# Quarter-array products with v in an attention and MLP kernel, with new product orders and a last product in three PSUM banks

## The chip, the core and the metric

One NeuronCore of a Trainium2 chip runs the whole program. The metric is the device time of one execution in microseconds (us), the median of several runs. Engines are named as the profile names them: PE (TensorE matmul), PEld (TensorE weight load), DVE (VectorE), ACT (ScalarE), SP (SyncE, which issues all DMAs here).

## The reference

Sigmoid attention over 8 batches and 12 heads of 448 positions and 64 dimensions, then an MLP with a sigmoid-gated activation over the 3584 tokens (768 wide, 2048 hidden):

```python
def _attn_ref(q, k, v):
    S = q.shape[2]                                  # q, k, v: (8, 12, 448, 64)
    scores = 1.0 / np.sqrt(64) * np.matmul(q, k.transpose(0, 1, 3, 2)) - np.log(S)
    attn = 1.0 / (1.0 + np.exp(-scores))
    return np.matmul(attn, v).astype(np.float32)

def _moe_ref(x, w_in, w_out):                       # w_in (768, 2048), w_out (2048, 768), both float64
    h = x @ w_in
    g = h * (1.0 / (1.0 + np.exp(-1.702 * h)))
    return (g @ w_out).astype(np.float32)
```

## The kernel before

The kernel is straight-line code. A planner (`Plan.run`) holds all tasks with their costs and dependencies, takes tasks engine by engine in the order in which they could begin, and so writes an instruction order for PE, ACT, DVE and SP; each engine then works its list in order, waiting on semaphores.

**Attention** comes first. Heads are taken in pairs (64 dimensions each, so two heads fill 128 partitions), and two pairs make a unit; there are 24 units. In a unit (`attention`, from L665) PE does, for each of the two pairs, three chunks of 128 key positions: `scores` (L568, matmuls L578), each chunk into one PSUM tile of two banks, one bank per head. ACT takes the sigmoid of each tile (L564). The last 64 key positions of both pairs share one tile: `scores_left` (L586, L594), on 64x64 quarters of the array. Then come the products with v: `values` (L601, L609) takes all 128 key positions of a chunk in one pass of 128 rows by 64 columns, the two heads side by side in the two column halves, and adds up the three chunks of one pair in one bank of a tile; `values_left` (L615, L622) adds the last 64 positions to it on quarters. One copy of 896 columns (`to_x`, L639, by ACT at L646 or by DVE at L647) takes the tile of two banks out, and SP stores it to DRAM.

PSUM has four tiles of two banks in this stage, q0 to q3, used in turn: a unit takes eight places (`held_ += 8`), seven for scores and one for the products with v, so a score tile waits for the reader of the tile four places earlier.

Beside this DVE and ACT round q and k to a leading and a remaining part (`round_and_rest`, L443 to L449), and decode the 64-bit weights (`decode`, L488 to L507).

**The first block** of 512 tokens (`first_block`) is an ordinary MLP: `up(n)` makes hidden tiles h in q0 (the second in q1), ACT the activation (`graw`, L829), and `down(n)` adds products o_q into q1, q2, q3, in that order of column groups.

**The other six blocks** are done three at a time (`triple`), each with a scheme of 20 products per matrix on sums of inputs (`SEQUENCES` lists the 40 products of a triple, as (matrix, product)). A product is 36 matmuls of 512 columns (L773) into one of two PSUM tiles of four banks, h0 and h1, in turn. DVE and ACT round its input into a pair (`gp`, `xp`, L987 to L999), seed its tile from a sum so far (L1087, L1089), copy it out (L1129) or add it up (L1163). The last product of all is copied to the output one column group at a time (`store`, L1195), from one tile.

Of the kernel before, what the change touches and what calls it, by code (L numbers as in the profile page):

```python
# [19 lines left out]
P = 128  # L20
# [8 lines left out]
    pair=2, wsplit=4, q0=1, q1=1, q2=1, q3=1, h0=1, h1=1,  # L29
# [10 lines left out]

SIGNAL, DRAIN, OVERLAP = 0.05, 0.17, {"ACT": 0.1, "DVE": 0.08}
# [10 lines left out]
SEQUENCES = ([(0, 19), (0, 8), (0, 10), (0, 18), (0, 2), (0, 16), (0, 12), (0, 1), (0, 14), (0, 15), (0, 11), (0, 7), (0, 17), (0, 4), (0, 0), (0, 5), (1, 8), (0, 9), (0, 3), (1, 4), (1, 12), (0, 13), (1, 3), (1, 18), (0, 6), (1, 16), (1, 9), (1, 10), (1, 2), (1, 19), (1, 14), (1, 15), (1, 17), (1, 7), (1, 1), (1, 13), (1, 11), (1, 0), (1, 5), (1, 6)], [(0, 18), (0, 19), (0, 14), (0, 10), (0, 3), (0, 12), (0, 13), (0, 2), (0, 1), (0, 5), (0, 11), (0, 17), (0, 7), (0, 9), (0, 15), (0, 0), (0, 6), (1, 2), (1, 9), (1, 0), (0, 16), (1, 3), (0, 4), (1, 5), (0, 8), (1, 10), (1, 16), (1, 4), (1, 15), (1, 8), (1, 13), (1, 19), (1, 17), (1, 12), (1, 1), (1, 6), (1, 18), (1, 14), (1, 11), (1, 7)])  # L52
# [15 lines left out]
class Task:  # L68
    def __init__(self, emits, costs, deps):
        self.emits, self.costs, self.deps = emits, costs, list(deps)  # L70
        self.ready, self.left, self.then, self.key = 0.0, 0, [], None
        self.begun, self.alone = False, True
        self.holds, self.landing, self.anytime, self.spare = [], LANDING, False, 0


class Buffer:
    def __init__(self):
        self.users, self.tile, self.until, self.slot, self.open, self.kind = [], None, 0.0, None, 0, None


class Plan:
# [3 lines left out]
    def buffer(self, tag):  # L85
        b, ring = Buffer(), self.rings.setdefault(tag, [])
        b.turn = len(ring) % BUFS[tag]
        ring.append(b)
# [11 lines left out]
    def either(self, costs, emits, deps=(), uses=()):  # L100
        t = Task(emits, costs, deps)
        for b in dict.fromkeys(uses):
            b.users.append(t)
        self.tasks.append(t)
        return t

    def run(self, streams):
# [43 lines left out]
        def since(t):  # L151
            when = t.ready
# [21 lines left out]
        def pe():  # L174
            if current:
                return (None if current[0].left else max(free["PE"], current[0].ready)), None
# [6 lines left out]
            for s, unit, due in heads:  # L183
# [4 lines left out]
                for t in first:  # L188
                    when = max(when, t.ready - before)
# [7 lines left out]
        while count < len(self.tasks):  # L197
# [4 lines left out]
            for i, (e, pool) in enumerate(pools.items()):  # L202
                pools[e] = pool = [t for t in pool if not t.begun]
                if pool:
                    options.append((max(free[e], min(since(t) for t in pool)), i + 1, e))
# [8 lines left out]
            else:  # L214
                now = [t for t in pools[e] if since(t) <= when]
# [4 lines left out]
                    if c.key < min(t.key, doing + SOON) and since(c) < when + PATIENCE * t.costs[e]  # L220
                ]
                if soon:
                    t = min(soon, key=lambda t: t.key)
                    when = max(when, since(t))
# [16 lines left out]
            else:  # L241
                free[e] = end - OVERLAP[e]
            for b in t.holds:
# [82 lines left out]
def sigmoid_attention_mlp(ctx: ExitStack, tc: tile.TileContext, qk, v, w, out):  # L326
# [62 lines left out]
    def make(b, tag, shape, dtype, name):  # L389
# [4 lines left out]
        if tag in ("h0", "h1") and tag not in spaces:  # L394
            for t in ("q1", "q0") if tag == "h0" else ("q3", "q2"):
                psum[t].close()
            banks(tag, "left" if tag == "h0" else "right")
        if late:
# [62 lines left out]
    def decode(n):  # L461
# [18 lines left out]
        plan.early.append((load, firsts[min(2 + pair, len(firsts) - 1)]))  # L480
# [87 lines left out]
    def scores(n, c, t_s, s, place):  # L568
# [14 lines left out]
        t = task("PE", (0.7, 0.61, 0.61)[c] if n else 0.9, emit, t_s, [ps, s])  # L583
        return t, sigmoid(f"a{n}_{c}", a, ps, t), a

    def scores_left(n, sources, place):  # L586
# [12 lines left out]
        t = task("PE", 0.8, emit, [t for ts, _ in sources for t in ts], [ps, *(b for _, b in sources)])  # L599
        return t, sigmoid(f"a{n}_{NC}", a, ps, t, "al"), a  # L600

    def values(n, c, t_a, a, t_v, vr, ps):

        def emit():
            if ps.tile is None:
                make(ps, ps.tag, [P, 2, 512], F32, f"av{n}")
            for j, cols in enumerate(halves_of_rows):
                at = ((n % 2 * 2 + j) * NC + c) * D
                nc.tensor.matmul(  # L609
                    ps.tile[cols, n % 2, :S], lhsT=vr.tile[:, at : at + D], rhs=a.tile[:, j],  # L610
                    start=c == 0, stop=False, skip_group_check=True,
                )

        return task("PE", (0.8, 0.75, 0.75)[c], emit, [t_a, t_v], [ps, a, vr])

    def values_left(t_a, a, t_v, vr, ps):
# [659 lines left out]
```

## Time and profile before

| | us |
|---|---|
| median of 3 runs | 1055.24 (1053.51 to 1055.38) |
| span of the profiled execution | 1051.2 |
| PE busy | 1038.1 (99%) |
| DVE busy | 841.9 (80%) |
| ACT busy | 552.7 (53%) |
| DMA, mean over the span | 258 GB/s |

The span is the time from the first to the last instruction of the one execution that was profiled; no device time of that execution is given beside it, so the 4.0 us between the span and the median are taken to lie around the span in every run. Busy shares are means over the span, and a wait by PE is what its busy time leaves out.

### The profile page before, as it was taken

The numbers are of one execution on the slowest core, as the hardware profiler recorded it, in microseconds if no ns is written. First come the engines' busy times: TensorE is split into PE (matmuls) and PEld (weight loads), VectorE is DVE, ScalarE is ACT, GpSimd is POOL, SyncE is SP. The second block draws the span as 40 slices with busy tenths as digits, with TensorE's granted clock in tenths as the row PEclk, the third lists the DMA queues.
The fourth block names the chain that finished last, engine by engine and source line by source line (L and its number), as shares of the span: only waits on it lengthen the run. The fifth ranks groups of instructions, "written<-read, shape, count | busy, mean of one in ns | idle before, by whom it ended". The sixth has DMA issues, their size and how long they took to land.

```text
span 1051.2 us, 13595 instructions
## 1 busy us (share of the span) xinstructions
PE 1038.1 (99%) x5300; PEld 778.9 (74%) x5300; DVE 841.9 (80%) x741; ACT 552.7 (53%) x512; POOL 0.2 (0%) x4
## 2 busy tenths in 40 slices
PE   9999999999999999999999999999999999999997
PEld 5545555555788888888887888888888888788886
DVE  5989789873999766788998989999875596888784
ACT  7888788886564423533554434342443263434342
POOL 0000000000000000000000000000000000000000
PEclk9999999999999999999999999999999999999999
DMA  9999988973999996757556666959766545545765
GB/s 358 388 377 361 342 312 308 344 262 135 336 401 373 372 383 225 256 186 243 193 176 219 233 198 196 295 197 372 274 222 199 184 147 180 153 148 158 234 203 186
DMA packets 114704, 271.44 MB, mean 258 GB/s; under 512 B 10320, under 2 KB 80080, under 8 KB 112592
## 3 DMA queue, kind: packets, MB, share of 16 engines
q1 hardware_dynamic: 114640, 270.57, 73.4%
q8 instruction: 42, 0.69, 0.3%
q14 instruction: 22, 0.18, 0.1%
HBM read 185.60 MB, written 84.93 MB: 257 GB/s over the span
## 4 chain that ended last, share of the span: by engine, by line
PE 91%; DVE 3%; DMA 3%; ACT 2%; issue 1%; SPq 0%; ACTq 0%; DVEq 0%
PE p L773 55%; PE av L609 11%; PE sc L578 9%; PE h L773 6%; PE o_q L773 6%; PE av L622 2%; PE sc L594 2%; DMA c<-wc 1%; ACT gp L987 1%; DVE o L1130 1%; SPq L417 0%; DVE gp L999 0%; DVE gs L716 0%; ACT o L1129 0%; DMA qkraw<-qk 0%
## 5 line engine op out<-in xcount | busy, mean ns | idle before, releaser
L773 PE MATMUL p<-gp,w 128*128 128x512 f32 x1440 | 329.2, 389 | 2.5 <-DVE gp L999 1.1
L773 PE MATMUL p<-xp,w 128*128 128x512 f32 x1440 | 327.8, 389 | 1.0 <-DVE xp L999 1.0
L773 PEld LDWEIGHTS p<-gp,w 128*128 128x128 f32 x1440 | 269.8, 188 | 60.6 <-DVE gp L999 2.0
L773 PEld LDWEIGHTS p<-xp,w 128*128 128x128 f32 x1440 | 270.2, 188 | 57.5 <-DVE xp L999 1.4
L564 ACT ACTIVATE a<-sc,bias 128x896 f32<-128x896 f32 x168 | 153.6, 1025 | 17.9 <-PE sc L578 17.9
L609 PE MATMUL av<-a,vraw 128*64 128x448 f32 x576 | 113.5, 543 | 0.0
L578 PEld LDWEIGHTS sc<-qk 64*128 64x128 f32 x846 | 77.7, 184 | 23.3 <-issue 16.2
L609 PEld LDWEIGHTS av<-a,vraw 128*64 128x64 f32 x576 | 39.2, 137 | 72.6 <-issue 49.5
L578 PE MATMUL sc<-qk 64*128 64x448 f32 x846 | 92.0, 368 | 0.9 <-DVE qk L449 0.9
L999 DVE TENSOR_TENSOR gp<-h,gp 128x2048 fp32r<-128x2048 f32 x31 | 70.9, 2288 | 9.2 <-ACT gp L987 8.8
L1129 ACT COPY h<-p 128x2048 f32<-128x2048 f32 x18 | 33.7, 1874 | 82.6 <-PE p L773 53.2
L773 PE MATMUL o_q<-g,w 128*128 128x512 f32 x288 | 66.5, 389 | 1.2 <-ACT graw L829 1.2
L773 PE MATMUL h<-x,w 128*128 128x512 f32 x288 | 66.6, 390 | 1.0 <-ACT x L646 1.0
L987 ACT CAST gp<-h 128x2048 fp32r<-128x2048 f32 x23 | 44.0, 1913 | 43.5 <-PE p L773 36.2
L1163 DVE TENSOR_TENSOR h<-h,p 128x2048 f32<-128x2048 f32 x23 | 52.1, 2284 | 17.6 <-PE p L773 10.4
L773 PEld LDWEIGHTS h<-x,w 128*128 128x128 f32 x288 | 54.0, 188 | 13.0 <-ACT x L646 1.8
L773 PEld LDWEIGHTS o_q<-g,w 128*128 128x128 f32 x288 | 54.0, 188 | 12.8 <-ACT graw L829 1.6
L1129 ACT COPY o<-p 128x1536 f32<-128x1536 f32 x18 | 25.9, 1443 | 59.5 <-PE p L773 19.2
L449 DVE TENSOR_TENSOR qk<-qkraw,qk 128x896 fp32r<-128x896 f32 x47 | 50.9, 1089 | 6.7 <-ACT qk L443 5.9
L716 DVE TENSOR_TENSOR h<-h,h 128x2048 f32<-128x2048 f32 x24 | 54.7, 2284 | 0.1
L736 ACT CAST wc<-ws 128x384 fp32r<-128x384 f32 (+1 forms) x57 | 32.1, 579 | 39.5 <-DVE ws L716 25.3
L987 ACT CAST xp<-x 128x1536 fp32r<-128x1536 f32 x19 | 28.1, 1480 | 39.2 <-PE p L773 31.4
(108 smaller groups left out, 969.9 us busy)
## 6 DMA issues: line engine op xcount, KB each, us to landing
w<-c SPq DMA_DIRECT2D x140, 384.0 KB, 4.3
w<-c SPq DMA_DIRECT2D x52, 768.0 KB, 4.7
w<-w SPq DMA_DIRECT2D x16, 1536.0 KB, 9.7
c<-wc SPq DMA_DIRECT2D x56, 384.0 KB, 5.6
qkraw<-qk SPq DMA_DIRECT2D x47, 448.0 KB, 6.4
vraw<-v SPq DMA_DIRECT2D x24, 448.0 KB, 6.5
c<-wc SPq DMA_DIRECT2D x14, 768.0 KB, 7.1
c<-w SPq DMA_DIRECT2D x28, 384.0 KB, 3.9
```

Source lines behind the costliest of these rows:

```text
L449: lambda: nc.vector.tensor_tensor(lo(), src(), hi().bitcast(F32), op=ALU.subtract),
L564: nc.scalar.activation(a.tile, ps.tile[:, :, :S], AF.Sigmoid, bias=bias, scale=scale)
L578: nc.tensor.matmul(ps.tile[:, j, :S], lhsT=src[kk][rows, S + c * P : S + (c + 1) * P], rhs=src[qq][rows, :S], start=i == 0, stop=i == len( ...
L594: nc.tensor.matmul(ps.tile[cols, j, :S], lhsT=src.tile[rows, S + NC * P :], rhs=src.tile[rows, :S], start=True, stop=True, skip_group_chec ...
L609: nc.tensor.matmul(ps.tile[cols, n % 2, :S], lhsT=vr.tile[:, at : at + D], rhs=a.tile[:, j], start=c == 0, stop=False, skip_group_check=True,)
L716: return task("DVE", cost, lambda: nc.vector.tensor_tensor(out(), x(), y(), op=op), deps, uses)
L736: t_hi = on_either((act(n), lambda: nc.scalar.copy(into()[:, 0], node.view())), (cast(n), lambda: nc.vector.tensor_copy(into()[:, 0], node ...
L773: nc.tensor.matmul(ps, lhsT=ws[:, a, c * P : (c + 1) * P], rhs=x[:, d, k], start=start and i == 0 and j == 0, stop=stop and i == len(todo) ...
L987: t_hi = on_either((act(n), lambda: nc.scalar.copy(part(0)(), node.view())), (cast(n), lambda: nc.vector.tensor_copy(part(0)(), node.view())),
L999: nc.vector.tensor_tensor(part(1)(), node.view(), part(0)().bitcast(F32), op=ALU.subtract)
L1129: t = on_either((act(self.n), lambda: nc.scalar.copy(view(), node.view())), (dve(self.n), lambda: nc.vector.tensor_copy(view(), node.view())),
L1163: nc.vector.tensor_tensor(view(), x.view(), y.view(), op=ALU.add if s0 == s else ALU.subtract)
```

## The change

Five things are changed.

1. **Quarters.** `values` now issues four matmuls of 64x64 for a chunk: the two halves of its 128 key positions go through the two row halves of the array, into the two banks of a tile. So each pair of heads has a PSUM tile of its own, with two partial sums. `values_left` moves in before the last two chunks, and adds to one bank of each tile.
2. **Taking out.** `to_x` now does, for each of the two tiles, an ACT copy of one bank (448 columns) and a DVE addition of the other bank to it. A unit takes nine PSUM places in place of eight.
3. **The planner** has new costs for these tasks, lets engines that touch the same PSUM tile take turns (`clear`), and gives the weight loads a later rank.
4. **Orders.** New `SEQUENCES` for the two triples; in the first block the o_q column groups go to q2, q3, q1 in place of q1, q2, q3; in the first unit `scores_left` goes between the scores of the two pairs.
5. **The last product** goes into three PSUM tiles of one bank each (z0, z1, z2), each seeded by an ACT instruction, and each copied out by itself (`end`).

```diff
     def values(n, c, t_a, a, t_v, vr, ps):
-            for j, cols in enumerate(halves_of_rows):
-                at = ((n % 2 * 2 + j) * NC + c) * D
-                nc.tensor.matmul(
-                    ps.tile[cols, n % 2, :S], lhsT=vr.tile[:, at : at + D], rhs=a.tile[:, j],
-                    start=c == 0, stop=False, skip_group_check=True,
-                )
-        return task("PE", (0.8, 0.75, 0.75)[c], emit, [t_a, t_v], [ps, a, vr])
+            for h, rows in enumerate(halves_of_rows):
+                for j, cols in enumerate(halves_of_rows):
+                    at = ((n % 2 * 2 + j) * NC + c) * D
+                    nc.tensor.matmul(
+                        ps.tile[cols, h, :S], lhsT=vr.tile[rows, at : at + D], rhs=a.tile[rows, j],
+                        start=c == 0, stop=c == NC - 1 and (n % 2 == 1 or h == 1), skip_group_check=True,
+                    )
+        return task("PE", 0.76, emit, [t_a, t_v], [ps, a, vr])
...
     def to_x(b, p, ends, pair):
+        for k, (t, ps) in enumerate(zip(ends, pair)):
+            def lower(k=k, ps=ps):
+                rows()
+                nc.scalar.copy(xb.tile[:, k], ps.tile[:, 1, :S])
+            c = task("ACT", act(S), lower, [t], [xb, ps])
+            done.append(task("DVE", dve(S), lambda k=k, ps=ps: nc.vector.tensor_tensor(
+                xb.tile[:, k], ps.tile[:, 0, :S], xb.tile[:, k], op=ALU.add), [c], [xb, ps]))
...
-            held_ += 8
-            ps = two_banks(held_)
+            held_ += 9
+            pair = [two_banks(held_ - 1), two_banks(held_)]
...
-            unit = [*run, left[0], *both]
+            unit = [*run, left[0], *both] if n > 1 else [*run[:NC], left[0], *run[NC:], *both]
...
-                for c, (tag, at) in enumerate((("q1", 0), ("q1", 1), ("q2", 0), ("q2", 1), ("q3", 0), ("q3", 1))):
+                for c, (tag, at) in enumerate((("q2", 0), ("q2", 1), ("q3", 0), ("q3", 1), ("q1", 0), ("q1", 1))):
...
+            def end(self, r, tag):
...
+                for i in range(NJ):
+                    bank = buffer(f"z{i}")
...
+                    t = task("ACT", act(T), seed, [*acc.done, *over], [bank, acc.b])
...
+                done = products(self.m, r, g_sums, G_SUMS[1], GB, NJ, 1, (None, tag, True), [], apart)
```

What PE does from the last scores of the second unit on, before (sc are score tiles, a their sigmoids, av the tile of the products with v, L594 and L622 the quarters for the last 64 positions):

```order
L578 MATMUL sc_2_377<-qk_3_320 128x448 x6
L594 MATMUL sc_3_389<-qkraw_2_232 64x448 x2
L594 MATMUL sc_3_389<-qkraw_3_234 64x448 x2
L609 MATMUL av_397<-a_0_347,vraw_2_244 64x448 x2
L609 MATMUL av_397<-a_1_366,vraw_2_244 64x448 x2
L609 MATMUL av_397<-a_2_375,vraw_2_244 64x448 x2
L609 MATMUL av_397<-a_0_386,vraw_2_244 64x448 x2
L609 MATMUL av_397<-a_1_395,vraw_2_244 64x448 x2
L609 MATMUL av_397<-a_2_405,vraw_2_244 64x448 x2
L622 MATMUL av_397<-a_3_415,vraw_2_244 64x448 x4
```

The products with v were of one form and the quarters of another around them. The same place on PE now:

```order
L593 MATMUL sc_2_390<-qk_3_302 128x448 x6
L609 MATMUL sc_3_400<-qkraw_2_230 64x448 x2
L609 MATMUL sc_3_400<-qkraw_3_232 64x448 x2
L626 MATMUL av_407<-a_0_357,vraw_2_234 64x448 x4
L626 MATMUL av_407<-a_1_369,vraw_2_234 64x448 x4
L626 MATMUL av_407<-a_2_387,vraw_2_234 64x448 x4
L626 MATMUL av_433<-a_0_398,vraw_2_234 64x448 x4
L639 MATMUL av_407<-a_3_422,vraw_2_234 64x448 x2
L639 MATMUL av_433<-a_3_422,vraw_2_234 64x448 x2
L626 MATMUL av_433<-a_1_405,vraw_2_234 64x448 x4
L626 MATMUL av_433<-a_2_431,vraw_2_234 64x448 x4
```

A matmul of this list is two instructions on the chip. Everything from `scores_left` to the end of the unit is now of the 64x64 form, there are two av tiles, and the first is complete two groups before the end.

What DVE now does around the end of a later unit (x_2_0 is the result of a unit, its av tiles the two that PE filled; x_0_768 is input of the first block, read back from DRAM; w and expo belong to the decoding of weights):

```order
L464 TENSOR_TENSOR qk_3_1029<-qkraw_3_905,qk_3_1029 128x896
L517 TENSOR_SCALAR w_13_1059<-w_13_924 128x1536
L499 TENSOR_SCALAR expo_1065<-w_13_924 128x1536
L671 TENSOR_TENSOR x_2_0_1067<-av_1023,x_2_0_1067 128x448
L464 TENSOR_TENSOR x_0_768<-x_0_768 128x1536
L671 TENSOR_TENSOR x_2_0_1067<-av_1049,x_2_0_1067 128x448
L515 TENSOR_TENSOR expo_933<-expo_933,sign_931 128x1536
```

Each unit now has two such additions (L671) on DVE, each behind an ACT copy (L668); the second can stand behind work of another kind.

The end of the program on ACT, before (p_4_7 is the last product's tile, o its output):

```order
L1129 COPY o_4_7972<-p_4_14_7878 128x1536
L1089 ACTIVATE p_4_7_7983<-o_2_7620 128x1536
L1195 ACTIVATE o_2_8035<-p_4_7_7983 128x512 x3
```

Seed, matmuls and copies were of one tile. The same place on ACT now (p_4_14_0 to p_4_14_2 are the three banks):

```order
L762 CAST w_4_14_0_8360<-w_4_14_0_8360 128x768
L1155 ACTIVATE p_4_14_0_8384<-o_4_7816 128x512
L762 CAST w_4_14_1_8362<-w_4_14_1_8362 128x768
L1155 ACTIVATE p_4_14_1_8399<-o_4_7816 128x512
L1155 ACTIVATE p_4_14_2_8402<-o_4_7816 128x512
L1167 ACTIVATE o_4_8433<-p_4_14_0_8384 128x512
L1167 ACTIVATE o_4_8433<-p_4_14_1_8399 128x512
L1167 ACTIVATE o_4_8433<-p_4_14_2_8402 128x512
```

The seed and the copies are of a tile per column group now, where one tile served all three.

## Rows read from the trace of the kernel before

**Rows 1.** Page: the span; busy time of PE, its share and instructions.
```profile
span 1051.2 us, 13595 instructions
PE 1038.1 (99%) x5300; PEld 778.9 (74%) x5300; DVE 841.9 (80%) x741; ACT 552.7 (53%) x512; POOL 0.2 (0%) x4
```

**Rows 2.** Waits of PE over the whole span: us in total, times, longest.
```profile
PE o_q L773 <- ACT graw L829: 1.2, 1, 1.2
PE p L773 <- DVE gp L999: 1.1, 2, 0.9
...
PE h L773 <- ACT x L646: 1.0, 1, 1.0
PE p L773 <- DVE xp L999: 1.0, 1, 1.0
PE sc L578 <- DVE qk L449: 0.9, 1, 0.9
PE p L773 <- ACT o L1195: 0.7, 1, 0.7
PE p L773 <- DMA w<-c: 0.6, 1, 0.6
```

**Rows 3.** A stretch of the attention: us, busy time (instructions) of each engine, clock, DMA share, GB/s.
```profile
26.00:208.00 182.00, 182.00 (x1350) 95.02 (x1350) 159.29 (x168) 154.44 (x159) 0.00 (x0) 1.00 0.93 347
```

**Rows 4.** PE timeline of one attention unit: start, us, instructions.
```profile
61.79 0.98 PE L594 MATMUL sc<-qkraw 64*64 64x448 f32 x8
62.71 4.73 PE L609 MATMUL av<-a,vraw 128*64 128x448 f32 x24
67.37 0.98 PE L622 MATMUL av<-a,vraw 64*64 64x448 f32 x8
68.28 3.91 PE L578 MATMUL sc<-qk 64*128 64x448 f32 x36
72.12 0.98 PE L594 MATMUL sc<-qkraw 64*64 64x448 f32 x8
```

**Rows 5.** Weight loads (PEld) in the same unit.
```profile
63.13 0.14 PEld L609 LDWEIGHTS av<-a,vraw 128*64 128x64 f32 x2 [0.23 <-issue]
...
66.52 0.14 PEld L609 LDWEIGHTS av<-a,vraw 128*64 128x64 f32 x2 [0.23 <-issue]
67.36 0.21 PEld L622 LDWEIGHTS av<-a,vraw 64*64 64x64 f32 x8 [0.70 <-ACT sign L488]
```

**Rows 6.** L622's matmuls in two short stretches of that unit.
```profile
67.35:67.75 0.40, 0.38 (x4) 1.00 1.11 367
67.75:68.25 0.50, 0.50 (x8) 1.00 1.36 338
```

**Rows 7.** PE timeline of the first unit.
```profile
3.94 3.31 PE L578 MATMUL sc<-qkraw 64*128 64x448 f32 x12
8.15 2.09 PE L578 MATMUL sc<-qk 64*128 64x448 f32 x18 [0.90 <-DVE qk L449]
...
16.66 3.90 PE L578 MATMUL sc<-qk 64*128 64x448 f32 x36
```

**Rows 8.** Groups by line and shape: busy us, mean ns; idle before, releasers.
```profile
L1195 ACT ACTIVATE o<-p 128x512 f32<-128x512 f32 x3 | 1.7, 595 | 13.8 <-PE p L773 13.8
L646 ACT COPY x<-av 128x896 f32<-128x896 f32 x12 | 10.9, 908 | 22.1 <-PE av L622 22.1
L647 DVE COPY x<-av 128x896 f32<-128x896 f32 x12 | 13.1, 1089 | 5.5 <-PE av L622 5.5
L739 DVE TENSOR_TENSOR wc<-ws,wc 128x384 fp32r<-128x384 f32 x48 | 25.5, 551 | 0.7 <-ACT wc L736 0.6
L507 DVE SCALAR_TENSOR_TENSOR w<-w,expo 128x1536 f32<-128x1536 f32 x16 | 28.0, 1751 | 0.1
```

**Rows 9.** Timeline of the end, PE and ACT.
```profile
1042.69 3.01 PE L773 MATMUL p<-gp,w 128*128 128x512 f32 x12 [0.75 <-ACT o L1195]
1045.74 1.09 ACT L1195 ACTIVATE o<-p 128x512 f32<-128x512 f32 x2 [3.10 <-PE p L773]
```

More of the change, by code (lines that the diff above doesn't have):

```diff
@@ L87, in buffer @@
         b.turn = len(ring) % BUFS[tag]
+        b.bank = tag in BANKS
         ring.append(b)
@@ L149, in run, with clear, since @@
         at, current, doing = [0, 0], [], 0
-        def since(t):
-            when = t.ready
+        def clear(t, e):
+            return max([end for b in t.banks for by, end in b.busy.items() if by != e], default=0.0)
+        def since(t, e):
+            when = max(t.ready, clear(t, e))
             if "SP" in t.costs and t.key > doing + PRESSING:
@@ L242, in run @@
                 free[e] = end - OVERLAP[e]
+            for b in t.banks:
+                b.busy[e] = max(b.busy.get(e, 0.0), end + SIGNAL)
             for b in t.holds:
@@ L397, in make @@
             banks(tag, "left" if tag == "h0" else "right")
+        if tag[0] == "z" and "z0" not in spaces:
+            psum[last_of[0]].close()
+            banks("z0", "left" if last_of[0] == "h0" else "right")
+            spaces["z1"] = spaces["z2"] = spaces["z0"]
         if late:
@@ L479, in decode @@
         load.landing += 1.5
-        plan.early.append((load, firsts[min(2 + pair, len(firsts) - 1)]))
+        plan.early.append((load, firsts[min(4 + pair, len(firsts) - 1)]))
         def exponent():
@@ L689, in attention @@
             if n % 2:
-                left = scores_left(n, [first, (t_q, qkr)], held_ + 7)
-            chunks = [scores(n, c, [t_s] if n else t_q[: c + 1], s, held_ + 1 + n % 2 * NC + c) for c in range(NC)]
+                left = scores_left(n, [first, (t_q, qkr)], held_ + (7 if n > 1 else NC + 1))
+            at = held_ + 1 + n % 2 * NC + (n == 1)
+            chunks = [scores(n, c, [t_s] if n else t_q[: c + 1], s, at + c) for c in range(NC)]
             if n % 2 == 0:
@@ L859, in first_block @@
             down(n)
-        for k in range(2):
+        for k in (1, 0):
             b = plan.slot()
@@ L1178, in store @@
             k, n = divmod(i, 3)
-            into, bank = out[one + n, k * NJ : (k + 1) * NJ].rearrange("j p t -> p j t"), node
-            parts = [slice(0, NJ)]
+            into = out[one + n, k * NJ : (k + 1) * NJ].rearrange("j p t -> p j t")
+            b, view, done = node.b, node.view, node.done
             if kind == "psum":
-                last = one + 3 == NB and all(left < 0 for left in nets[1].left.values())
-                parts = [slice(j, j + 1) for j in range(NJ)] if last else parts
@@ L1184, in store @@
                 b, view = nets[1].slot(("out", i))
-                node, ends = Node(b, view, []), node.each if last else node.done
+                if sign > 0:
+                    done = [on_either((act(XB), lambda: nc.scalar.copy(view(), node.view())),
+                                      (dve(XB), lambda: nc.vector.tensor_copy(view(), node.view())), done, [b, node.b])]
+                else:
+                    done = [task("ACT", act(XB), lambda: nc.scalar.mul(view(), node.view(), -1.0), done, [b, node.b])]
@@ L1219, in triple @@
             places[i] = onto
-            nets[m].product(r, onto)
+            if one + 3 == NB and i == len(sequence) - 1:
+                plan.rings[onto[1]].pop()
+                nets[m].end(r, onto[1])
+            else:
+                nets[m].product(r, onto)
         return [u for p in sequence for u in units_of[p]]
```

144 lines of the change are left out of this document (80 added, 64 removed).

## The prediction

> **What bounds the kernel now.** I read the page first, then the waits of PE, then timelines of PE at the places that the change touches. The page gives PE 1038.1 of 1051.2 us [rows 1]; what is left is 13.1 us. The waits of PE explain about half of it: eight short ones, among them 1.0 before the first h product, 1.2 before the first o_q product, 0.9 in the first unit and 0.7 in the last product [rows 2]; most of the rest is the end, after PE's last matmul at about 1045.7 (42.69 plus 3.01) [rows 9]. In the attention, from 26 to 208 us, PE is busy for all of 182 us, with the clock at its full 2.4 GHz (granted 1.00) [rows 3]. So nothing that DVE, ACT or DMA do there ends a wait of PE, and a gain must come out of PE's own work, or out of the named waits.
>
> The timeline of one unit shows where PE's work has slack [rows 4]. From one `scores_left` to the next (61.79 to 72.12) a unit takes 10.33 us. Between 61.79 and 68.28, 6.49 us, stand 0.92 for the scores of the last 64 positions, 4.66 for the 24 instructions of `values`, and 0.91 for the eight of `values_left`, each counted from start to start.
>
> **What a change of form costs.** Within `values` the loads of weights step in pairs, ten rows from 63.13 to 66.52, so 3.39 us for nine steps, 0.377 each [rows 5]: two column halves run beside each other for 0.377 us. Twelve such steps are 4.52, and 4.66 is 0.14 more. The quarters of `values_left` are eight instructions in 0.91 us. Four of them run in the first 0.40 us of that group, and all eight are in flight in the next half [rows 6], so four run beside each other; two steps of 0.377 are 0.754, and 0.91 is 0.16 more. I read the 0.14 to 0.16 as the price of changing from one form of matmul to another, and take 0.15.
>
> **The change, part by part.**
>
> *Quarters.* A chunk was four instructions in two steps of two; it becomes eight in two steps of four. That halves nothing: the columns that stream are the same, so a chunk keeps 0.754 us if the steps stay at 0.377. What goes is changes of form. `scores_left`, six chunks and `values_left` are now one run of eight groups of the 64x64 form: 8 x 0.754 + 0.15 = 6.18 us against 6.49, a gain of 0.31 a unit. In 23 units (the first has another order) it is 7.1 us. Bounds of a group in the run: 0.754 from below, since no row shows a faster step, and 0.91 from above, the group that stands alone [rows 4]. I take the lower end: the eight loads of a group start and end within 0.21 us [rows 5], which a step of 0.377 a half can cover. The two ends go into the range and into a rival.
>
> The Trainium skill speaks against more and smaller matmuls: "TensorEngine Tiling (Array Packing)", section Instruction Overhead, gives about 60 cycles of overhead for each. By an estimate from that page, 25 ns at 2.4 GHz for each of the 576 added instructions would be 14.4 us if they were paid one after another, and the sum would come out slower than before. The group that stands alone does not bear this out: its eight instructions take 0.16 us over two steps, and the 24 of the other form take 0.14 over twelve [rows 4].
>
> *First unit.* PE waits 0.90 us there for the first rounded q and k, from about 7.25 to 8.15 [rows 7]. `scores_left` needs only loaded q and k, not rounded ones, and is put into this gap: 0.9 us.
>
> *The first h product* waits 1.0 us for the copy of the last av tile, because both use q0 [rows 2]. With nine places a unit the last two tiles stand in q0 and q1, and the one in q0 is complete two groups, 1.5 us, before the attention ends. ACT needs 0.54 for its copy (595 ns for 512 columns [rows 8], less 64 columns at about 0.83) and DVE 0.62 for its addition (between 551 ns at 384 columns and 1089 at 896 [rows 8]), 1.2 together; q0 is free in time. Gain 1.0 us.
>
> *The first o_q product* waits 1.2 us for `graw` [rows 2], the activation that reads h from q1, where o_q began. It now begins in q2. Gain 1.2 us.
>
> *The last product.* PE stops 0.75 us between its second and third column groups, for ACT's copy out of the same tile, and after PE's last matmul ACT makes two copies in 1.09 us, the first of which could not start before [rows 9]. With a tile per group the stop goes, 0.7, and one copy of 0.60 stays after the end: 0.5 less. The seeds are three ACT instructions of 0.6 [rows 8] and lie beside the product before. Gain 1.2 us, provided that the pair and the weights of the last product, now rounded behind two additions on DVE, are ready.
>
> *Taking out.* A unit gets two copies on ACT (1.08) and two additions on DVE (1.24), and loses one copy, which alternated between ACT at 908 ns and DVE at 1089 [rows 8]: 0.45 and 0.54 on the mean. ACT rises by 0.63 a unit, DVE by 0.70. Before, ACT is busy 154.4 and DVE 159.3 of 182 us [rows 3], 8.76 and 9.03 in a unit of 10.33; now 9.4 and 9.7 in a unit of 10.02. Both still fit, so I cost this at nothing; the cover is 0.6 us of ACT and 0.3 of DVE a unit. If it is gone, PE waits at the fourth score tile of the next unit, which takes the place of the second av tile.
>
> *New orders.* In the triples PE waits 2.7 us in all (1.1 for gp, 1.0 for xp, 0.6 for a load [rows 2]). The number of products and matmuls is the same. What another order makes of these waits the trace can't show: from below all 2.7 may go, from above I take two more waits in each of the two triples, of the longest that PE has, 1.2 [rows 2], 4.8 in all. I take no change, since it is nearer to what the old order shows. The later rank of the weight loads I cost at nothing: DVE's decoding has no reader on PE until the first block.
>
> **Sum.** 7.1 + 0.9 + 1.0 + 1.2 + 1.2 = 11.4 us off a span of 1051.2: 1039.8. The median lies 4.0 us above the span, so 1043.8 us, 1.1% under 1055.24. What tells from no change is 0.2%, 2.1 us.
>
> **Rivals.**
>
> *Some of the gain goes to late additions.* Between the end of a unit and its successor's fourth score tile lie three score tiles, half of the 3.84 us of a unit's scores [rows 4], so 1.92 us. Copy and addition take 1.16 and some 0.2 for signals, and leave 0.56. One decoding instruction of 1.75 us on DVE [rows 8] that gets between, or a wait for a DMA like that of x_0, makes PE 1.2 us late. For it: two engines now stand in the way where one did, DVE would be at 97%, and DMA has a share of 0.93 [rows 3]. Against it: the order is written with the tiles' turns in mind, and the first tile is ready early. At four such waits it is 4.8 us, 1048.6. A rule of the same page of the Trainium skill, section PSUM Bottleneck, says as much: tiling speeds up TensorE and not the emptying of PSUM. No row of before shows it as a bound.
>
> *Slower: the same, in most units.* At 0.5 us a unit (11.4 over 23) the gain is gone. With 1.2 us in two units of three, 15 of 23, it is 18 us and the time 1061.8. It needs DVE to be late nearly always; its busy share of 88% [rows 3] speaks against.
>
> *Slower: quarters don't pack.* If a group in a run costs what it does alone, 0.91, a unit loses 8 x 0.91 - 6.49 = 0.79, 23 units 18.2 us, and with 4.3 us of the other gains the time is 1069.1. It decides from a group of 0.83 us (6.49 and 4.3/23, over eight). The two steps in [rows 6] speak against it.
>
> *Slower: added instructions are paid for.* Eight loads of quarters take 0.21 us, 0.026 each [rows 5]. If each of the 576 added ones (24 units, six chunks, four more) lay open on PE, it would be 15.0 us: 1058.8. For it: twice as many instructions. Against it: in the group that stands alone all eight together cost no more than a change of form. It is the way in which the Trainium skill's rule on instruction overhead would act here.
>
> *The orders matter.* Worse by 4.8 us: 1048.6. Better by 2.7: 1041.1.
>
> **How the numbers follow.** The forecast with small waits, 1041.5 to 1046.5: 0.60. Late additions in some units, 0.15, new orders worse, 0.10, both around 1048.6. Orders better, 1041: 0.09. Late additions in most units 0.02, quarters that don't pack 0.02, added instructions that are paid for 0.02. The range takes in the forecast, the better orders with a lower run, and the two cases at 1048.6 with a little more: 1039.5 to 1050.5. Faster by over 0.2%: 0.60 + 0.15 + 0.10 + 0.09 less 0.01, so 0.93. Slower: the 0.06, less 0.01 that stays near no change, 0.05. Same: 0.02.
>
> **What would show it.** PE's timeline should show a run of 64 instructions of the 64x64 form in each unit of the attention, about 6.2 us from its start to the next scores, and units of about 10.0 us. The waits of PE for ACT x, graw and ACT o should be gone from the list, the one for the first rounded q and k too. After PE's last matmul there should be one ACT copy of 0.6 us. PE's wait for a score tile's place, named by DVE x, would show late additions; seven us and more for that run would show quarters that don't pack; and waits for gp, xp or loads between 390 and 1035 us beyond 2.7 us would show that the orders cost more than they did. The prediction is wrong if units stay above 10.2 us.

## The result and the profile after

The changed kernel takes 1045.99 us, the median of four runs (1042.55 to 1048.22), against 1055.03 of four runs of the kernel before (1053.51 to 1055.38): a ratio of 0.9918, 95% interval 0.9904 to 0.9932. The forecast was 1043.8 with a range of 1039.5 to 1050.5. Total and direction came out about as forecast; several of the terms behind them did not.

From the page of the changed kernel:

```profile
span 1040.8 us, 14831 instructions
...
PE 1032.8 (99%) x5876; PEld 784.3 (75%) x5876; DVE 863.7 (83%) x792; ACT 552.9 (53%) x537; POOL 0.2 (0%) x4
...
L626 PE MATMUL av<-a,vraw 64*64 64x448 f32 x1152 | 117.8, 539 | 0.0
...
L671 DVE TENSOR_TENSOR x<-av,x 128x448 f32<-128x448 f32 x48 | 29.9, 624 | 28.4 <-ACT x L668 28.1
```

Against [rows 1], the span is 10.4 us shorter and PE has 576 more instructions, yet is busy for 5.3 us less. The profiled execution is the fastest of the four runs: its device time is 1042.55, so 1.75 us lie around its span.

The waits of PE after, in the columns of [rows 2]:

```profile
PE still L390 <- DVE bias L393: 1.0, 1, 1.0
PE sc L593 <- DVE qk L464: 1.0, 2, 0.7
PE sc L593 <- DVE x L671: 0.5, 1, 0.5
```

The waits for graw, for ACT x, for ACT o, for gp, for xp and for a load are gone. One is new: the wait for DVE x is for the place of an av tile.

PE's timeline of one undisturbed unit after, as [rows 4] for before:

```profile
56.82 3.92 PE L593 MATMUL sc<-qk 64*128 64x448 f32 x36
60.68 0.98 PE L609 MATMUL sc<-qkraw 64*64 64x448 f32 x8
61.57 3.24 PE L626 MATMUL av<-a,vraw 64*64 64x448 f32 x32
64.63 0.93 PE L639 MATMUL av<-a,vraw 64*64 64x448 f32 x8
65.38 1.68 PE L626 MATMUL av<-a,vraw 64*64 64x448 f32 x16
66.99 0.47 PE L593 MATMUL sc<-qk 64*128 64x448 f32 x2
```

The 64 instructions of the 64x64 form stand in one run, as forecast. Start to start the unit takes 10.17 us (56.82 to 66.99), the run 6.31 of it. Forecast were 10.02 and 6.18.

Where the 10.4 us of the span came from, by start times in the two traces (before, after; us):

| stretch of PE | before | after | gain | forecast |
|---|---|---|---|---|
| unit 1 | 12.72 | 12.26 | 0.5 | 0.9 |
| units 2 to 24, up to the first h product | 238.60 | 235.40 | 3.2 | 8.1 |
| first h product to first product of the triples | 132.18 | 130.69 | 1.5 | 1.2 |
| triples, to PE's last matmul | 658.27 | 653.38 | 4.9 | 0.7 |
| PE's last matmul to the end of the span | 5.5 | 5.1 | 0.4 | 0.5 |

The attention gave less than half of what was forecast, and the triples, whose new orders were costed at nothing, gave most.

PE where the attention ends and the first block begins, after:

```profile
249.98 1.68 PE L626 MATMUL av<-a,vraw 64*64 64x448 f32 x16
251.59 16.61 PE L799 MATMUL h<-x,w 128*128 128x512 f32 x72
268.05 2.20 PE L799 MATMUL o_q<-g,w 128*128 128x512 f32 x9
```

Neither the first h nor the first o_q product has a wait in front. ACT at the end of the program, after (before: [rows 9]):

```profile
1030.27 0.60 ACT L1167 ACTIVATE o<-p 128x512 f32<-128x512 f32 x1 [5.05 <-PE p L799]
1032.99 0.60 ACT L1167 ACTIVATE o<-p 128x512 f32<-128x512 f32 x1 [2.12 <-PE p L799]
1035.70 0.60 ACT L1167 ACTIVATE o<-p 128x512 f32<-128x512 f32 x1 [2.12 <-PE p L799]
```

The three copies of the last product lie 2.7 us apart, each behind its own column group, and one of 0.60 stays after PE.

Not every unit takes 10.16. Of units 2 to 23, in this trace, five take 10.34, 10.77, 10.67, 10.43 and 10.36, which is 1.8 us over five times 10.16. Here is a late one: PE, then DVE, then ACT, from the timeline of 96 to 104 us.

```profile
97.66 2.12 PE L593 MATMUL sc<-qk 64*128 64x448 f32 x18
100.23 2.09 PE L593 MATMUL sc<-qk 64*128 64x448 f32 x18 [0.46 <-DVE x L671]
...
97.89 1.75 DVE L520 SCALAR_TENSOR_TENSOR w<-w,w 128x1536 f32<-128x1536 uint32 x1
99.56 0.62 DVE L671 TENSOR_TENSOR x<-av,x 128x448 f32<-128x448 f32 x1
...
96.69 1.69 ACT L503 ACTIVATE sign<-w 128x1536 bf16<-128x1536 int16 x1
98.22 0.58 ACT L668 COPY x<-av 128x448 f32<-128x448 f32 x1
```

ACT copies the second av tile only behind an instruction of the decoding, DVE's addition stands behind another, and the fourth score tile of the next unit, which takes that tile's place, waits for the addition. The same five units are late in the other traces of this kernel, so that part is in the order as written.

### The profile page after: what moved, and what is told of

Read it like the earlier page. It is cut to its first block, busy times and chain, and to the rows that moved or that the text cites. A ratio compares the mean times of both kernels' runs of the same rounds, so it can differ in the third digit from the quotient of the medians.

```text
span 1040.8 us, 14831 instructions
## 1 busy us (share of the span) xinstructions
PE 1032.8 (99%) x5876; PEld 784.3 (75%) x5876; DVE 863.7 (83%) x792; ACT 552.9 (53%) x537; POOL 0.2 (0%) x4
## 4 chain that ended last, share of the span: by engine, by line
PE 94%; DVE 2%; ACT 1%; DMA 1%; issue 1%; SPq 0%; ACTq 0%; DVEq 0%
PE p L799 63%; PE av L626 9%; PE sc L593 7%; PE h L799 6%; PE o_q L799 6%; PE sc L609 2%; PE av L639 1%; DMA qkraw<-qk 0%; DVE x L671 0%; ACT a L579 0%; DMA xd<-x 0%; ACT sign L503 0%; DVE w L522 0%; DVE qk L464 0%; DVE w L520 0%
## 5 line engine op out<-in xcount | busy, mean ns | idle before, releaser
L626 PE MATMUL av<-a,vraw 64*64 64x448 f32 x1152 | 117.8, 539 | 0.0
L626 PEld LDWEIGHTS av<-a,vraw 64*64 64x64 f32 x1152 | 42.2, 133 | 68.0 <-issue 48.3
L1197 ACT COPY h<-p 128x2048 f32<-128x2048 f32 x23 | 42.9, 1877 | 82.5 <-PE p L799 79.9
L1026 DVE TENSOR_TENSOR gp<-h,gp 128x2048 fp32r<-128x2048 f32 x27 | 61.8, 2287 | 6.8 <-ACT gp L1014 6.4
L1014 ACT CAST gp<-h 128x2048 fp32r<-128x2048 f32 x17 | 32.6, 1915 | 58.3 <-PE p L799 56.7
L799 PEld LDWEIGHTS o_q<-g,w 128*128 128x128 f32 x288 | 54.1, 188 | 11.2
L671 DVE TENSOR_TENSOR x<-av,x 128x448 f32<-128x448 f32 x48 | 29.9, 624 | 28.4 <-ACT x L668 28.1
L1231 DVE TENSOR_TENSOR o<-o,p 128x1536 f32<-128x1536 f32 x18 | 31.3, 1751 | 13.9 <-PE p L799 12.9
```

Of the source, the lines that this page charges most:

```text
L626: nc.tensor.matmul(ps.tile[cols, h, :S], lhsT=vr.tile[rows, at : at + D], rhs=a.tile[rows, j], start=c == 0, stop=c == NC - 1 and (n % 2 = ...
L671: done.append(task("DVE", dve(S), lambda k=k, ps=ps: nc.vector.tensor_tensor(xb.tile[:, k], ps.tile[:, 0, :S], xb.tile[:, k], op=ALU.add), ...
L799: nc.tensor.matmul(ps, lhsT=ws[:, a, c * P : (c + 1) * P], rhs=x[:, d, k], start=start and i == 0 and j == 0, stop=stop and i == len(todo) ...
L1014: t_hi = on_either((act(n), lambda: nc.scalar.copy(part(0)(), node.view())), (cast(n), lambda: nc.vector.tensor_copy(part(0)(), node.view())),
L1026: nc.vector.tensor_tensor(part(1)(), node.view(), part(0)().bitcast(F32), op=ALU.subtract)
L1197: t = on_either((act(self.n), lambda: nc.scalar.copy(view(), node.view())), (dve(self.n), lambda: nc.vector.tensor_copy(view(), node.view())),
```

## The experiments

Two questions were open. Why does an undisturbed unit take 10.16 us and not 10.02? And what in the triples gave 4 us: the orders, or the turns in the planner?

**The changed kernel again (e1_again).** No edit.

> The changed kernel as it is, to see where its runs differ. Theory: units without a late addition take 10.16 us each, and runs differ by how many units wait at the fourth score tile for a late addition on DVE; 2 to 8 us more than the 235.4 us of the first profile for units 2 to 24 in a slower run, with the triples' 653.4 us from first to last product the same within 0.5. Rival: the runs differ in the triples, by loads that come late or by the clock, and the 235.4 us stay.

1043.85 us (six runs, 1042.38 to 1048.04), ratio 0.9911, interval 0.9895 to 0.9928. The units of its trace repeat those above within 0.1 us, the late ones too; unit 1 takes 11.36 where it took 12.26, and one wait for a weight load (0.9) stands ahead of a product of the triples. That trace is again of one of the faster runs (1042.67), so it doesn't show where the slower ones have their time; e11 below does. The kernel before, measured beside it, spreads over 2.7 us (1052.97 to 1055.66), this one over 5.7.

**Halves in place of quarters (e2_halves).** The products with v and the taking out as before; all else as changed.

```diff
-            for h, rows in enumerate(halves_of_rows):
-                for j, cols in enumerate(halves_of_rows):
...
+            for j, cols in enumerate(halves_of_rows):
+                at = ((n % 2 * 2 + j) * NC + c) * D
+                nc.tensor.matmul(
+                    ps.tile[cols, n % 2, :S], lhsT=vr.tile[:, at : at + D], rhs=a.tile[:, j],
...
-            held_ += 9
+            held_ += 8
```

> Products with v again in 128x64 form, one tile and one copy a unit; orders, planner, first block and last product as changed. Theory: units take 10.33 us again, each without a wait, so units 2 to 24 take 237.5 us against 235.4 and the run is some 2 us slower than a good run of the changed kernel, and no slower than its slower runs; triples 653.4 as in the changed kernel. Rival (quarters carry the gain): 7 us slower or more, near 1050.

1045.72 us (1045.45 to 1049.16), ratio 0.9926, interval 0.9913 to 0.9938. Its units take 10.33 us again (all but two of units 2 to 23, in a trace of its slowest run), so the step to 10.16 belongs to the quarters. Between the fastest runs of this kernel and of e1 they are worth 3.1 us (1045.45 less 1042.38), between the medians 1.9, and the intervals of the two ratios overlap. Most of the change's gain is there without its quarters.

**Shorter sigmoids (e7_short_sigmoid).** From the first scores of an undisturbed unit to its first product with v it is 4.75 us before and 4.75 after, though the change of form between them is gone. The first av tile takes the place of the fourth score tile. If the sigmoid of that tile ends just when PE is ready to go on, a shorter sigmoid must let the 0.1 out.

```diff
-            nc.scalar.activation(a.tile, ps.tile[:, :, :S], AF.Sigmoid, bias=bias, scale=scale)
+            nc.gpsimd.memset(a.tile[:, :, S - 64 :], 0.5)
+            nc.scalar.activation(a.tile[:, :, : S - 64], ps.tile[:, :, : S - 64], AF.Sigmoid, bias=bias, scale=scale)
```

> Each sigmoid leaves out the last 64 of 448 columns of each head (GpSimd fills them with a constant), so one takes 0.92 us in place of 1.02. Theory: the first group of the products with v waits for the sigmoid of the fourth scores, whose PSUM tile it takes; with sigmoids 0.1 us shorter that wait goes, the step from the first scores of a unit to its first product with v falls from 4.75 to 4.65 us, and an undisturbed unit from 10.16 to 10.02. Rival: 10.16 is what the instructions of PE cost by themselves, and units keep it.

Weight loads at the end of a unit's scores, first in the changed kernel, then in this one:

```profile
60.68 0.21 PEld L609 LDWEIGHTS sc<-qkraw 64*64 64x64 f32 x8 [0.30 <-ACT a L579]
61.57 0.21 PEld L626 LDWEIGHTS av<-a,vraw 64*64 64x64 f32 x8 [0.68 <-ACT a L579]
```

```profile
60.25 0.21 PEld L610 LDWEIGHTS sc<-qkraw 64*64 64x64 f32 x8 [0.31 <-issue]
60.71 0.18 PEld L627 LDWEIGHTS av<-a,vraw 64*64 64x64 f32 x4 [0.25 <-issue]
61.05 0.15 PEld L627 LDWEIGHTS av<-a,vraw 64*64 64x64 f32 x4 [0.17 <-issue]
```

In the changed kernel the first eight loads for the products with v end an idle time that the sigmoid (ACT a) ended. With shorter sigmoids nothing is waited for, and four of the eight loads are made early, beside the matmuls of `scores_left`. First scores to first product is 4.64 now, the undisturbed unit 10.01 us: the forecast's 10.02. ACT's fourth sigmoid of a unit says the same, first in the kernel before (the unit of [rows 4], products with v from 62.71 on), then in the changed kernel (products from 61.57 on):

```profile
61.56 1.01 ACT L564 ACTIVATE a<-sc,bias 128x896 f32<-128x896 f32 x1
```

```profile
60.49 1.02 ACT L579 ACTIVATE a<-sc,bias 128x896 f32<-128x896 f32 x1
```

Before, it ends at 62.57 and the products start 0.14 us later; now it ends at 61.51 and they start 0.06 later. In the trace of the changed kernel that gap is 0.05 in 17 of units 2 to 24; with shorter sigmoids it is 0.36 and more in all of them. So the quarters took up what slack there was and met the sigmoid. The sigmoids also come later than they did: in the units shown the fourth ends 4.69 us after the unit's first scores, not 4.62, and why is not shown. The late units stay (five of 10.5 to 11.2 us), so the whole, which leaves out the sigmoid of 64 of 448 columns, gains little: 1044.29 in two runs, ratio 0.9908, interval 0.9884 to 0.9932.

**The old orders (e3_old_orders).** `SEQUENCES` of the kernel before, all else as changed.

```diff
-SEQUENCES = ([(0, 15), (0, 16), (0, 19),
...
+SEQUENCES = ([(0, 19), (0, 8), (0, 10),
...
```

> Only the two lists of products are those of before; the planner with turns at PSUM tiles stays. Theory: the new orders took the waits for gp, xp and a load out of the triples, so 2.7 to 4 us come back there, 656 to 657.5 from first to last product, and the time is 3 to 4 us over the changed kernel's. Rival: the planner's turns did it, and the old orders under the new planner cost under 1 us.

1051.74 us (eleven runs), ratio 0.9972, interval 0.9962 to 0.9983: 7.9 us over the changed kernel (e1), where 3 to 4 were expected. In the traces the triples take 658.20 us against 653.38, with one wait of 2.9 for a weight load; before they took 658.27, with the stop of the last product in it. The first block takes 132.64 against 130.69, behind waits for ACT w (0.8) and DVE w (0.5). Another 4.4 us of this profiled execution lie in one unit. Its ACT, DVE and PE:

```profile
77.59 1.48 ACT L458 CAST x<-x 128x1536 fp32r<-128x1536 f32 x1 [3.11 <-DMA xd<-x]
...
79.53 0.62 DVE L671 TENSOR_TENSOR x<-av,x 128x448 f32<-128x448 f32 x1 [1.98 <-ACT x L668]
...
80.21 0.89 PE L593 MATMUL sc<-qk 64*128 64x448 f32 x6 [1.12 <-DVE x L671]
82.41 3.18 PE L593 MATMUL sc<-qk 64*128 64x448 f32 x18 [1.31 <-DVE x L671]
```

An ACT cast that reads input back from DRAM stands ahead of the copy of an av tile, and waits 3.1 us for DMA. The copy, the addition and PE's next scores wait behind it; the second addition stands behind DVE's own 1.75 us on that input. This part is not owed to the old orders: the changed kernel has it too in e11 below.

**New orders without turns (e8_no_turns).**

```diff
         def clear(t, e):
-            return max([end for b in t.banks for by, end in b.busy.items() if by != e], default=0.0)
+            return 0.0
```

> New orders of products, but the planner lets engines use one PSUM tile at once as before. Theory: the orders were found with the turns, and what took the waits out of the triples is both together: without the turns 1 to 4 us come back from first to last product (653 to 654 in the changed kernel). Rival: the orders alone did it, and nothing changes within 0.7 us.

1059.57 us (1059.2 to 1061.81), ratio 1.0057, interval 1.0045 to 1.007: slower than the kernel before. The triples take 668.6 us, 15.2 more than in the changed kernel, where 1 to 4 were expected. PE's longest waits, then the stretch behind the longest with the busy time of each engine and the granted clock, then SP's queue around PE's longest wait:

```profile
PE p L799 <- DMA w<-c: 6.7, 1, 6.7
PE p L799 <- DVE gp L1026: 3.7, 2, 1.9
```

```profile
657.00:663.00 6.00, 5.63 (x14) 4.42 (x15) 5.97 (x5) 0.00 (x0) 0.00 (x0) 0.52 0.64 187
```

```profile
650.92 0.56 SPq L432 DMA_DIRECT2D c<-wc  x1
653.75 1.88 SPq L432 DMA_DIRECT2D w<-c  x3
```

and SP's waits from 640 to 656 us:

```profile
SPq L432 <- DVE w L765: 9.6, 1, 9.6
SPq L432 <- DMA c<-wc: 2.2, 1, 2.2
```

PE waits from about 650.7 to 657.4 for weights whose loads SP issues only from 653.75 on: SP had stood 9.6 us in front of a store (c<-wc), by the view for DVE's weights, and then 2.2 us until a store had landed. After the wait the clock is granted at 0.52, the lower level, for about six us, and matmuls of the triples start 0.427 us apart, not 0.227. So the new orders are worth nothing in the triples by themselves, nor are the turns (e3): the two gain together. That the planner, which writes the instruction order from them, places loads and their readers differently with and without turns is the likely reason; it is argued, not shown. The planner's new costs and the later rank of the weight loads are in both runs and were not tried apart.

**Later loads in the plan (e5_late_loads).** The planner counts the weight loads 4 us and the reloads of x 5 us later than it did, so that it puts their readers further back.

```diff
-        load.landing += 1.5
+        load.landing += 5.5
...
+        for d in t:
+            d.landing += 5.0
```

> The planner counts on weight loads 4 us later and on the reload of x from DRAM 5 us later, so DVE and ACT get to instructions that wait for a DMA later, behind the additions rather than ahead of them. Theory: the slower runs of the changed kernel (up to 6 us over its fastest) are runs in which such an instruction waits for a late DMA ahead of an addition; the spread falls under 3 us and the median comes to 1041.5 to 1043. Rival: the spread comes from loads of the triples or from elsewhere, and runs from 1042.5 to 1048 stay.

1043.36 us (1041.43 to 1044.21), ratio 0.9902, interval 0.9887 to 0.9917. All but one of the units 2 to 23 take 10.1 to 10.4 us, and the four runs lie within 2.8 us. The median is just above what was expected, and the interval overlaps that of the changed kernel, so a gain is not shown; the narrower spread would fit reloads that are waited for less often, but four runs don't settle it.

**ACT frees the second tile alone (e6_act_frees).** ACT copies both banks of the second av tile, and DVE adds them in SBUF. For this the result buffer grows by a half, and there are two of them, not three (not in the cut below).

```diff
+                if k:
+                    nc.scalar.copy(xb.tile[:, 1:3], ps.tile[:, :, :S])
...
+                done.append(task("DVE", dve(S), lambda: nc.vector.tensor_tensor(
+                    xb.tile[:, 1], xb.tile[:, 2], xb.tile[:, 1], op=ALU.add), [c], [xb]))
```

> ACT copies both banks of the second av tile out (896 columns, 0.91 us in place of 0.53) and DVE adds them in SBUF, so the fourth score tile of the next unit waits for ACT alone. Theory: the three units of the changed kernel that take 10.4 to 10.8 us since the addition stands behind a 1.75 us instruction come to 10.2, units 2 to 24 take 234 us against 235.4, 1 to 1.5 us less in all. Rival: ACT becomes the late one (9.8 of 10.16 us a unit), and units take 10.3 or more, 2 us or more slower than the changed kernel.

1050.64 us, ratio 0.9967, interval 0.9956 to 0.9979: slower than the changed kernel (0.9911 in e1), as the rival had it, where 1 to 1.5 us less were expected. Units 2 to 24 are 3.5 us longer than in the first trace of the changed kernel, first block and triples 2.5 and 1.4. ACT in one unit:

```profile
46.41 1.66 ACT L503 ACTIVATE sign<-w 128x1536 bf16<-128x1536 int16 x1
47.96 0.90 ACT L669 COPY x<-av 128x896 f32<-128x896 f32 x1
48.75 6.41 ACT L579 ACTIVATE a<-sc,bias 128x896 f32<-128x896 f32 x7
```

The longer copy pushes the row of sigmoids back: they begin 1.37 us after the unit's first scores (47.38), in the changed kernel 0.99 (56.82 and 57.81). First scores to first product is 5.1 us in such units and most units take 10.4 to 10.6. In all of units 2 to 24 the first product starts 0.05 us after the fourth sigmoid ends, whether that is 4.65 or 5.1 us after the first scores: the sigmoids set the start of the products with v. A version in which DVE adds both banks straight from PSUM, with no ACT copy ahead (e4), gave no time, so what that copy alone costs is open.

**The scores of the last 64 positions later (e9_left_later).** The first two groups of products with v go before `scores_left`, and so the first av tile takes the place of the third score tile, whose sigmoid is done earlier. On top of e5.

```diff
-                left = scores_left(n, [first, (t_q, qkr)], held_ + (7 if n > 1 else NC + 1))
+                left = scores_left(n, [first, (t_q, qkr)], held_ + (8 if n > 1 else NC + 1))
...
-            pair = [two_banks(held_ - 1), two_banks(held_)]
+            pair = [two_banks(held_ - (2 if n > 1 else 1)), two_banks(held_)]
...
-            unit = [*run, left[0], *both] if n > 1 else [*run[:NC], left[0], *run[NC:], *both]
+            unit = [*run, *both[:2], left[0], *both[2:]] if n > 1 else [*run[:NC], left[0], *run[NC:], *both]
```

> On top of the later loads: the scores of the last 64 positions go behind the first two groups of products with v, so these take the PSUM tile of the third scores, whose sigmoid is done 0.9 us earlier, and all of it stays of the 64x64 form. Theory: the wait that short sigmoids took away goes here too, undisturbed units take 10.02 us, units 2 to 24 some 232 us against 234.9, and the run is 2.5 to 3 us faster than with later loads alone, 1039 to 1040.5 at best. Rival: the first av tile is now due one score tile earlier in the next unit, late additions of both tiles stop PE, and units stay at 10.16 or more.

1041.5 us (1040.59 to 1042.64), ratio 0.9881, interval 0.9866 to 0.9896. PE in one unit:

```profile
56.65 3.90 PE L593 MATMUL sc<-qk 64*128 64x448 f32 x36
60.48 1.73 PE L626 MATMUL av<-a,vraw 64*64 64x448 f32 x16
62.03 0.93 PE L609 MATMUL sc<-qkraw 64*64 64x448 f32 x8
62.78 1.68 PE L626 MATMUL av<-a,vraw 64*64 64x448 f32 x16
64.29 0.93 PE L639 MATMUL av<-a,vraw 64*64 64x448 f32 x8
65.04 1.68 PE L626 MATMUL av<-a,vraw 64*64 64x448 f32 x16
66.65 0.67 PE L593 MATMUL sc<-qk 64*128 64x448 f32 x4
```

With no sigmoid shortened and no work left out, the run of 64 instructions takes 6.17 us (60.48 to 66.65) and the unit 10.00. Units 2 to 24 take 233.06 us, 2.3 less than in the changed kernel and 1 more than expected; what is left over is late additions (PE waits 1.2 us for DVE x). It is the fastest version here. Against e5, on which it builds, the median is 1.9 us lower and units 2 to 24 take 233.06 us, not 234.89, but the intervals of the two ratios overlap. Of the twelve runs of the changed kernel only two, of 1042.38 and 1042.55, are as fast as the slowest here, though the intervals of the two ratios just touch (0.9896 here, 0.9895 in e1).

**The last product in one tile (e10_one_tile_last)**, copied out and stored as a whole.

```diff
-            if one + 3 == NB and i == len(sequence) - 1:
+            if False:
```

> The changed kernel with its last product in one tile of four banks, copied out and stored as a whole. Theory: PE's last matmul comes at the same time, since the old stop was made by copying out group by group; after it a copy of 1.44 us stands in place of one of 0.60 and a store of 768 KB in place of 256 KB, so the end takes 6 to 7 us in place of 5.1 and the run is 1 to 2 us slower. Rival: three banks bring nothing, because the end hangs on other stores, and the time is the same within 0.5.

1047.59 us (1045.11 to 1048.86), ratio 0.9936, interval 0.9923 to 0.9949. The end, on ACT:

```profile
1038.48 1.45 ACT L1255 ACTIVATE o<-p 128x1536 f32<-128x1536 f32 x1 [10.71 <-PE p L799]
```

One copy of 1.45 us stays after PE instead of 0.60, and from PE's last matmul to the end of the span it is 6.1 us, not 5.1. This is the price of a whole copy at the end. The rest of the difference to the changed kernel lies elsewhere: two attention units of 11.2 and 11.1 us and a wait of 1.4 for a weight load, and the changed kernel has traces with such units (e12) and such a wait (e1) too.

**The changed kernel twice more (e11_again, e12_again).** They are to show where a slower run has its time.

> One more execution of the changed kernel, in the hope of a trace of one of its slower runs (the two traces so far are of its faster ones, 1042.6 and 1042.7). Theory: if the run is over 1045, its added time stands in a few units of the attention in which a DMA-bound instruction comes ahead of an addition, and in the wait for a load at the first products of the triples (0.9 us in the trace before), not in the rest of the triples. Rival: it stands elsewhere in the triples, or in every unit.

> The same once more: if it is over 1045, the same as for the run before; if not, units 2 to 24 take 235.4 us and the triples 653 to 654.

1047.81 and 1043.76 us. The spans are 5.2 and 1.2 us above that of the first trace. In the slower one unit 1 takes 13.00 us (12.26 in the first trace) and unit 8 takes 14.52 (10.34), while triples and first block are within 0.3 us. In the other it is unit 8 with 12.18. The slower one's ACT and PE in unit 8:

```profile
78.30 1.48 ACT L458 CAST x<-x 128x1536 fp32r<-128x1536 f32 x1 [3.18 <-DMA vraw<-v]
79.69 0.52 ACT L668 COPY x<-av 128x448 f32<-128x448 f32 x1
...
80.92 0.87 PE L593 MATMUL sc<-qk 64*128 64x448 f32 x6 [1.25 <-DVE x L671]
83.12 3.49 PE L593 MATMUL sc<-qk 64*128 64x448 f32 x18 [1.33 <-DVE x L671]
```

It is the place and the pattern of e3: a cast that waits over 3 us for input read back from DRAM (the view names the DMA that landed last), with the copy of an av tile queued behind it. Not all of the 4.4 us over an undisturbed unit is waiting. Behind the two waits (1.25 and 1.33) the clock falls to its lower level:

```profile
83.00:86.00 3.00, 2.88 (x16) 2.60 (x18) 3.00 (x4) 2.89 (x4) 0.00 (x0) 0.50 1.05 400
```

The last 18 instructions of these scores take 3.42 us (83.12 to 86.54). In e12, where unit 8 waits 0.30 and 1.33 and the clock stays up, they take 2.01: some 1.4 us are the clock's. In the slower of these traces the added time is here, and in unit 1 by when the rounded q and k are ready; the other slow runs have no trace.

## Why the prediction was right in total and wrong in its terms

**Quarters: mis-sized, 7.1 us forecast, about 2.2 in the trace** (3.2 for units 2 to 24, less 1.0 of the h wait). The price of a group was right: 0.75 us within the run, 6.17 for all eight in e9. So was what the changes of form cost in sum, since the undisturbed unit is 10.01 where nothing else is in the way (e7, e9). The step that failed stands in the first part: "PE is busy for all of 182 us ... So nothing that DVE, ACT or DMA do there ends a wait of PE". PE is shown as busy to the modelled ends of its matmuls, and a wait of 0.1 us is inside that. The products with v came 0.09 to 0.14 us after the fourth sigmoid before and come 0.05 after it now in undisturbed units, with the sigmoid itself some 0.07 later: taking a change of form away ahead of them uncovered that wait. Of the 0.31 us a unit, 0.17 came, 3.9 us in 23 units; late additions took 1.8 of it back.

**Taking out: costed at nothing, cost 1.8 us in the profiled execution and more in slower ones.** The step was "Both still fit, so I cost this at nothing". The busy shares do fit (ACT 165.8 and DVE 169.8 of the 182 us from 26 to 208 us); what isn't there is a free place at the right moment, in five units of 22. (DVE's 9.03 us a unit is 9.04 by [rows 3]; nothing hangs on it.) The first rival described it, down to the fourth score tile that waits, at 4.8 us for the whole kernel. It was real and smaller in the best run. In the slower one, unit 8 alone is 4.4 us over 10.16, some 1.4 of it by the lower clock that followed the waits, which the forecast had no term for.

**First unit: 0.9 forecast, 0.46 in the profiled execution.** `scores_left` stands in the gap, as said, but the rounded q and k came later, and PE still waits 0.7 for DVE qk. In the other three traces of the same kernel unit 1 takes 11.36, 11.61 and 13.00 us, so this term is not a constant.

**First h and o_q product: right.** The wait of 1.0 is gone, and o_q begins 16.45 us after h where it began after 17.81: 1.36 against 1.2 forecast.

**Last product: right.** The stop of 0.75 is gone and one copy of 0.60 is left at the end. From PE's end to the end of the span it is 5.1 us against 5.5, so 1.1 in all against 1.2.

**New orders and turns: costed at nothing, worth about 4 us in the triples** (4.9 less the stop of the last product). The step that failed is "I take no change, since it is nearer to what the old order shows". The bounds were not met either: from below all 2.7 us of waits could go, but a wait of PE costs more than its row shows. In the trace of before the steps around each wait in the triples are stretched too; all steps longer than 0.227 us add up to 5.3 us, 1.0 of them at the last product, and after the change to 0.4. I also took orders and turns as two things with one price each. They are one: in the triples the turns alone gain nothing (e3) and the orders alone lose (e8).

**Around the span: 4.0 us taken, 1.75 measured.** Every run that gives both shows 1.7 to 2.1. So most of what I read as an offset must have been an execution of before that was faster than its median. The changed kernel's profiled execution is 3.4 us under its own median (1042.55 and 1045.99), so from the span to the median it is 5.2 us.

The three wrong terms, minus 4.9 for the quarters, plus 4 for the orders and minus 0.4 for the first unit, nearly cancel: 10.4 us off the span where 11.4 were forecast. With 5.2 in place of 4.0 from the span to the median that makes the 2.2 us by which the forecast was low. A right total was no evidence for the working.

**The rivals on the slow side.** Quarters pack: a group is 0.75 us in a run. The added instructions are not paid for: twice the instructions of a chunk take the same time (eight in 0.75 us, where four took two steps of 0.377). By the estimate from the Trainium skill's "TensorEngine Tiling (Array Packing)", Instruction Overhead, 14.4 us were to be paid; the rows here show none of it.

## What to carry to other kernels

When a cost is to be taken out of an engine that is busy all the time, ask what else ends at the same moment: compare start to start in the trace with the time at which each operand and each PSUM place becomes free, since a wait of a tenth of a microsecond does not show as idle time. What frees a PSUM tile belongs ahead of work that depends on a DMA, on every engine that takes part: the late units show what it costs otherwise, though e5 does not show a gain from it. And an order is to be judged together with the planner that turns it into queues, by one run of each alone.

## What the hardware showed that was not expected

- A wait of TensorE of 0.1 us between two groups of matmuls is inside its busy time. First scores to first product with v took 4.75 us with a change of form between, 4.75 without it and 4.64 with a shorter sigmoid, and the list of PE's waits names none of these.
- After waits of 2.9 us (e3) and 6.7 us (e8) in the triples the clock was granted at the lower level: 0.57 and 0.52 on the mean of the stretches behind them. Matmuls of 512 columns then started 0.427 us apart, not 0.227, for some 7 and 12 steps, which adds 0.2 us each to what the wait itself took. Two waits of 1.25 and 1.33 us in one unit of the attention were followed by it too (e11, 0.50), waits of 0.30 and 1.33 in the same place were not (e12).
